# One semaphore increment per accumulation group instead of one per matmul, in a fused attention and feed-forward block

## The chip, the cores and the metric

The kernel runs on one core of a Trainium2 chip. The metric is the device time of one execution in microseconds; a quoted time is the median of several executions. Single looks (one execution) have no state of their own and are used only for distances inside their traces.

Distances between instructions are differences of start times in the instruction records of the trace. They are whole nanoseconds, so I give means.

## The reference, cut to what matters

```python
# x: 2048 x 1024; 32 query heads of 128, 4 key/value heads, the last 512 keys; F = 3584
mod = silu(c) @ w_mod                      # six vectors of 1024: sa, ca, ga, sb, cb, gb
h = layernorm(x) * (1 + ca) + sa
q = h @ wq;  p = softmax(q @ k^T * 128**-0.5);  o = p @ v
x = x + ga * (o @ wo)
h = layernorm(x) * (1 + cb) + sb
x = x + gb * ((silu(h @ w_gate) * (h @ w_up)) @ w_down)
```

## The kernel before

The kernel is written by hand, in program order per engine. A small tracker inserts every wait: each operation on an engine increments that engine's semaphore, and a buffer remembers the count at which it was last written and read. An engine that needs the buffer waits for that count.

```python
def op(self, st, emit, reads=(), writes=()):
    ...                                   # req: the counts that the buffers ask for
    for s, c in req.items():
        if s is st and st.self_exempt:    # TensorE does not wait for itself
            continue
        if synced.get(s, 0) >= c:
            continue
        eng.wait_ge(s.sem, c)
        synced[s] = c
    ins = emit()
    st.count += st.inc
    c = st.count
    ins.then_inc(st.sem, st.inc)
    for b in reads:
        b.reads[st] = c
    for b in writes:
        b.last_write = (st, c)
        b.reads = {}
```

All matmuls go through one helper, which is why nearly all of TensorE's work has one line number (L266) in the profile:

```python
def mm(out_ap, lhsT, rhs, start, stop, reads, bank_buf, skip=False):
    T.op(PE, lambda: TE.matmul(out_ap, lhsT, rhs, start=start, stop=stop, skip_group_check=skip),
         reads=reads, writes=[bank_buf])
```

The groups that the argument touches: the modulation at the start (one-column matmuls, a new weight each, accumulated over eight steps `k`), the scores (four matmuls that are whole groups by themselves), and P@V (groups of four, 129 columns: V and a column of ones that gives the softmax's denominator).

```python
# modulation, first half of the columns; later read by a copy on DVE
for k in range(kh * HK, (kh + 1) * HK):
    for pt in range(2):
        for j in range(HK):
            o = pt * HK + j
            mm(bank(XB, 1, 2 * o), w[:, k, j * P:(j + 1) * P], sc_bf[:, k:k + 1],
               k == 0 and o == 0, k == DT - 1, ...)
...
# scores of one head, then two exponentials of 128x1024 on ACT
for kt in range(KT):
    mm(bank(SCB + kt), kT_sb[:, gk * KT + kt, :], qT_s[qs], True, True, ...)
...
# P@V of one head; rows of v_aug are VW = 130 elements, 260 B, apart
for j in range(TPC):
    for kt in range(KT):
        mm(bank(b, P + 1, (j % 2) * 130), ex_s[es][:, kt, j * P:(j + 1) * P],
           v_aug[:, gk * KT + kt, 0:P + 1], kt == 0, kt == KT - 1, ...)
```

The Q and output projections and the feed-forward part are groups of 8, 32, 8 and 28 matmuls of 512 columns.

The softmax here doesn't subtract the row's maximum and nothing guards it: scores larger than these inputs give would overflow.

Of the kernel before, what the change touches and what calls it, by code (L numbers as in the profile page):

```python
# [39 lines left out]
class _Tracker:  # L40
# [11 lines left out]
            self.issuer_synced[key] = d  # L52
        return d

    def op(self, st, emit, reads=(), writes=()):
        req = {}
        for b in reads:
            lw = b.last_write
            if lw is not None:
                s, c = lw  # L60
                if req.get(s, 0) < c:
                    req[s] = c
        for b in writes:
            lw = b.last_write
            if lw is not None:
                s, c = lw
                if req.get(s, 0) < c:
                    req[s] = c
            for s, c in b.reads.items():
                if req.get(s, 0) < c:  # L70
                    req[s] = c
        synced = self._synced(st)
        eng = st.issuer
        for s, c in req.items():
            if s is st and st.self_exempt:
# [3 lines that stand above are left out]
            eng.wait_ge(s.sem, c)  # L79
            synced[s] = c  # L80
        ins = emit()
        st.count += st.inc
        c = st.count
        ins.then_inc(st.sem, st.inc)
        for b in reads:
            b.reads[st] = c
        for b in writes:
            b.last_write = (st, c)
            b.reads = {}
        return c  # L90
# [40 lines left out]
def bass_adaLN_cond__sliding_block_cached__swiglu_ffn__prompt_kernel(  # L131
# [124 lines left out]
    with nc.Block() as block:  # L256

        @block.gpsimd
        def _(g):
# [4 lines left out]

            def mm(out_ap, lhsT, rhs, start, stop, reads, bank_buf, skip=False):
                T.op(PE, lambda: TE.matmul(out_ap, lhsT, rhs, start=start, stop=stop, skip_group_check=skip),  # L266
                     reads=reads, writes=[bank_buf])

            def transpose(out_ap, in_ap, reads, bank_buf):
                T.op(PE, lambda: TE.transpose(out_ap, in_ap, ident),  # L270
# [12 lines left out]
            def finish(gen):  # L283
                while gen in bg:
# [6 lines left out]
                 reads=[B_ident], writes=[B_ident])  # L291
# [78 lines left out]
            for gk in range(Hkv):  # L370
                T.op(Q_k[gk], lambda: SP.dma_start(k_nat[:, gk * KT:(gk + 1) * KT, :],
                                                   A_k_cache[0, gk, Sk - W:Sk, :].rearrange("(p k) d -> p k d", p=P)),
                     writes=[B_kn[gk]])
            load_wq(1)
            for gk in range(Hkv):
                T.op(Q_v[gk], lambda: SP.dma_start(v_aug[:, gk * KT:(gk + 1) * KT, 0:P],
                                                   A_v_cache[0, gk, Sk - W:Sk, :].rearrange("(p k) d -> p k d", p=P)),
                     writes=[B_vg[gk]])
# [55 lines left out]
            def mod_mm(w_ap, wbuf, k, cols):  # L434
                for n, (j, o) in enumerate(cols):
                    mm(bank(XB, 1, 2 * o), w_ap[:, j * P:(j + 1) * P], sc_bf[:, k:k + 1],
                       k == 0 and n == 0, k == DT - 1, [wbuf, B_sc], PB[XB], skip=True)
# [10 lines left out]
            def warm(n, b):  # L448
                for _ in range(n):
                    mm(bank(b), zwarm[:, 0:P], zwarm, True, True, [B_zw], PB[b])  # L450
# [27 lines left out]
            def mod_slice(sl, kh):  # L478
                for k in range(kh * HK, (kh + 1) * HK):
                    for pt in range(2):  # L480
                        w = wme[sl][pt]
# [3 lines that stand above are left out]
                               k == 0 and o == 0, k == DT - 1, [B_wme[sl][pt][kh], B_sc], PB[XB], skip=True)  # L485
# [4 lines left out]
                 reads=[B_x[tl]], writes=[B_ns4[tl], B_acc])  # L490
            T.op(POOL, lambda: g.tensor_scalar(nmean[:, :], acc[:, 0:1], -1.0 / D, None, op0=ALU.mult),
                 reads=[B_acc], writes=[B_nm])
            T.op(ACT, lambda: A.activation(nsc4[tl], x_res[:, tl, :], AF.Square, bias=nmean[:, 0:1], accum_out=acc[:, 1:2]),
                 reads=[B_x[tl], B_nm], writes=[B_ns4[tl], B_acc])
# [10 lines left out]
                 reads=[B_acc], writes=[B_rs[tl]])  # L505
            T.op(POOL, lambda: g.tensor_tensor(rstd[tl][:, :], rstd[tl][:, :], mhalf[:, 0:1], ALU.pow),
                 reads=[B_rs[tl], B_mh], writes=[B_rs[tl]])
            T.op(POOL, lambda: g.tensor_tensor(nmr[:, :], nmean[:, :], rstd[tl][:, :], ALU.mult),
                 reads=[B_rs[tl], B_nm], writes=[B_nr])
            T.op(ACT, lambda: A.activation(nsc4[tl], x_res[:, tl, :], AF.Identity, bias=nmr[:, 0:1], scale=rstd[tl][:, 0:1]),  # L510
                 reads=[B_x[tl], B_nr, B_rs[tl]], writes=[B_ns4[tl]])
# [373 lines left out]
```

## Time and profile before

| | |
|---|---|
| time, median of 3 | 1291.36 us (1290.51 to 1291.66) |
| matmuls in the program | 7778: 5226 of 512 columns, 2048 of 129, 384 of one, 56 of 256, 64 of 128 |
| start-to-start distance, 512 columns | 215.8 ns |
| 256 columns | 109.2 ns |
| 129 columns (P@V) | 58.6 ns: 56.0 after the first of a group, 59.2 to 60.1 after the others |
| one column (modulation) | 25.6 ns |

The page of the kernel before opens with the span and the busy time of each engine. "PEld" is TensorE's weight load, which runs beside the matmuls.

```profile
span 1290.8 us, 17912 instructions
...
PE 1265.6 (98%) x7636; PEld 651.7 (50%) x7778; DVE 447.7 (35%) x823; ACT 341.3 (26%) x384; POOL 37.3 (3%) x94
```

PE is busy nearly all the time, but matmuls overlap in their pipeline, so that alone doesn't say that they run at their own pace. The groups of TensorE instructions, with shapes kept apart (columns: line, engine, operation, output and input, array and shape, count; busy us and mean ns of one; idle time before them and what ended it):

```profile
L266 PE MATMUL ps<-arena 128*128 128x512 bf16 x5084 | 1134.8, 380 | 10.9 <-DVE arena L467 2.2 <-ACT arena L620 0.6 <-DVE tmp L657 0.4
L266 PE MATMUL ps<-arena 128*128 128x129 bf16 x2048 | 140.6, 220 | 1.1 <-DVE arena L638 1.1
L266 PE MATMUL ps<-sc_bf,arena 128*128 128x1 bf16 x384 | 11.5, 164 | 0.0
```

A matmul of 512 columns lasts 380 ns, yet the next one starts 215.8 ns later. (142 of the 5226 have no record.) The distances times the counts give about 1269 us. The list of what TensorE waited for (total us, times, longest) is short:

```profile
PE ps L270 <- DVE nsc L399: 10.2, 1, 10.2
PE ps L266 <- DVE arena L467: 2.2, 2, 1.7
PE ps L266 <- DVE arena L638: 1.1, 1, 1.1
PE ps L266 <- ACT arena L620: 0.6, 2, 0.4
PE ps L266 <- DVE tmp L657: 0.4, 1, 0.4
```

The chain of work that ended last, in order of time (start, us, what): a piece of the start, where the second half of the modulation ends and DVE reads it; one of attention; and two of the feed-forward part.

```profile
23.23 1.48 PE ps L266 x33
24.74 0.17 DVE mod_bf L440
...
295.35 7.00 PE ps L266 x55
...
703.96 10.74 PE ps L266 x49
714.75 10.74 PE ps L266 x49
```

From one feed-forward piece to the next, 10.79 us pass for 50 matmuls: 215.8 ns each. The chain is TensorE all the way, so a change pays only if it changes the pace of matmuls or one of the few waits above.

### The profile page before, as it was taken

The numbers are of one execution on the slowest core, as the hardware profiler recorded it, in microseconds if no ns is written. First come the engines' busy times: TensorE is split into PE (matmuls) and PEld (weight loads), VectorE is DVE, ScalarE is ACT, GpSimd is POOL, SyncE is SP. The second block draws the span as 40 slices with busy tenths as digits, with TensorE's granted clock in tenths as the row PEclk, the third lists the DMA queues.
The fourth block names the chain that finished last, engine by engine and source line by source line (L and its number), as shares of the span: only waits on it lengthen the run. The fifth ranks groups of instructions, "written<-read, shape, count | busy, mean of one in ns | idle before, by whom it ended". The sixth has DMA issues, their size and how long they took to land.

```text
span 1290.8 us, 17912 instructions
## 1 busy us (share of the span) xinstructions
PE 1265.6 (98%) x7636; PEld 651.7 (50%) x7778; DVE 447.7 (35%) x823; ACT 341.3 (26%) x384; POOL 37.3 (3%) x94
## 2 busy tenths in 40 slices
PE   6999999999999999999999999999999999999999
PEld 3565545556445564456544444444444444444444
DVE  3455423654136542265422332233222331221222
ACT  2555402555015551055620111001100111001100
POOL 1001200000000000000000000000000000000000
PEclk9999999999999999999999999999999999999999
DMA  8989800844105541046340683045420564044300
GB/s 261 304 222 285 235 1 21 184 111 107 37 5 127 133 118 46 1 116 122 70 152 15 205 302 131 17 130 162 151 71 19 157 208 131 17 135 142 131 9 25
DMA packets 212592, 155.33 MB, mean 120 GB/s; under 512 B 104736, under 2 KB 199840, under 8 KB 211488
## 3 DMA queue, kind: packets, MB, share of 16 engines
q1 hardware_dynamic: 212512, 154.17, 42.4%
q8 instruction: 61, 1.00, 0.3%
q14 instruction: 19, 0.16, 0.0%
HBM read 125.83 MB, written 4.19 MB: 101 GB/s over the span
## 4 chain that ended last, share of the span: by engine, by line
PE 97%; issue 1%; DVE 1%; ACT 0%; DMA 0%; SPq 0%; POOL 0%; ACTq 0%
PE ps L266 97%; DMA x_res<-in_A_x_dram 0%; ACT arena L620 0%; PE ps L270 0%; DVE tmp L657 0%; DVE arena L467 0%; DVE st L388 0%; ACT L620 0%; ACT arena L489 0%; SPq L309 0%; DVE nsc L399 0%; DVE arena L638 0%; DVE x_res L659 0%; ACT arena L593 0%; DVE rl L635 0%
## 5 line engine op out<-in xcount | busy, mean ns | idle before, releaser
L266 PE MATMUL ps<-arena 128*128 128x512 bf16 (+1 forms) x7204 | 1251.5, 333 | 12.0 <-DVE arena L467 2.2
L266 PEld LDWEIGHTS ps<-arena 128*128 128x128 bf16 x7346 | 637.4, 98 | 624.9 <-issue 7.9
L620 ACT ACTIVATE arena<-ps 128x1024 bf16<-128x1024 f32 x256 | 261.7, 1023 | 358.9 <-PE ps L266 347.2
L815 ACT ACTIVATE arena<-ps 128x512 bf16<-128x512 f32 x112 | 66.9, 597 | 514.5 <-PE ps L266 511.6
L816 DVE TENSOR_TENSOR arena<-ps,arena 128x512 bf16<-128x512 f32 x112 | 77.5, 692 | 276.2 <-PE ps L266 276.2
L657 DVE TENSOR_TENSOR tmp<-ps,rowb 128x512 f32<-128x512 f32 (+1 forms) x65 | 44.4, 683 | 320.5 <-PE ps L266 320.5
L571 DVE CAST arena<-ps 128x512 bf16<-128x512 f32 x124 | 85.8, 692 | 65.5 <-PE ps L266 65.5
L638 DVE TENSOR_TENSOR arena<-ps,rl 128x512 bf16<-128x512 f32 x128 | 88.5, 691 | 4.4
L635 DVE RECIPROCAL rl<-ps 128x4 f32<-128x4 f32 x128 | 23.4, 183 | 149.7 <-PE ps L266 149.7
L388 DVE BATCH_NORM_STATS2 st<-x_res 128x6 f32<-128x512 bf16 x62 | 42.4, 684 | 4.3 <-DMA x_res<-in_A_x_dram 4.2
L393 POOL TENSOR_SCALAR rstd<-mv 128x1 f32<-128x1 f32 x31 | 7.0, 227 | 955.2 <-DVE mv L392 943.7
L659 DVE TENSOR_TENSOR arena<-tmp,x_res 128x512 bf16<-128x512 f32 (+1 forms) x33 | 22.3, 676 | 1.1
L659 DVE TENSOR_TENSOR x_res<-tmp,x_res 128x512 bf16<-128x512 f32 x32 | 22.1, 692 | 1.1
L404 DVE TENSOR_SCALAR arena<-arena,gain,mod_bf 128x512 bf16<-128x512 bf16 x56 | 20.4, 406 | 0.0
L395 POOL TENSOR_TENSOR rstd<-rstd,mhalf 128x1 f32<-128x1 f32 x31 | 17.7, 572 | 2.6
L399 DVE TENSOR_SCALAR nsc<-x_res,mv,rstd 128x1024 bf16<-128x1024 bf16 x30 | 16.1, 536 | 2.1 <-POOL rstd L395 2.1
L270 PE MATMUL ps<-arena,nsc 128*128 128x128 bf16 x16 | 2.1, 311 | 10.4 <-DVE nsc L399 10.2
L266 PEld LDWEIGHTS ps<-sc_bf,arena 128*128 128x128 bf16 x384 | 11.3, 97 | 0.5
L266 PE MATMUL ps<-sc_bf,arena 128*128 128x1 bf16 x384 | 11.5, 164 | 0.0
L540 POOL TENSOR_SCALAR arena<-arena,c 128x128 bf16<-128x128 bf16 x16 | 9.7, 621 | 36.0 <-PE ps L266 35.9
L392 DVE BATCH_NORM_AGGREGATE mv<-st 128x2 f32<-128x12 f32 x31 | 6.5, 209 | 1.1
L270 PEld LDWEIGHTS ps<-arena,nsc 128*128 128x128 bf16 x16 | 1.5, 142 | 10.4 <-DVE nsc L399 10.4
(37 smaller groups left out, 30.9 us busy)
## 6 DMA issues: line engine op xcount, KB each, us to landing
arena<-in_A_wq_dram SPq DMA_DIRECT2D x31, 1024.0 KB, 5.9
arena<-in_B_w_gate_dram SPq DMA_DIRECT2D x28, 1024.0 KB, 5.3
arena<-in_B_w_up_dram SPq DMA_DIRECT2D x28, 1024.0 KB, 7.4
arena<-in_w_mod_dram SPq DMA_DIRECT2D x8, 1024.0 KB, 7.2
arena<-in_A_wo_dram SPq DMA_DIRECT2D x8, 1024.0 KB, 8.2
arena<-in_B_w_down_dram SPq DMA_DIRECT2D x7, 1024.0 KB, 6.3
arena<-in_w_mod_dram SPq DMA_DIRECT2D x8, 512.0 KB, 7.8
out_dram<-arena SPq DMA_DIRECT2D x15, 256.0 KB, 2.0
```

What stands on the lines that cost most here:

```text
L266: T.op(PE, lambda: TE.matmul(out_ap, lhsT, rhs, start=start, stop=stop, skip_group_check=skip), reads=reads, writes=[bank_buf])
L388: T.op(DVE, lambda: V.bn_stats(st_[sl][:, hf * 6:hf * 6 + 6], x_res[:, t, hf * 512:hf * 512 + 512]), reads=[B_x[t]], writes=[B_st[sl]])
L395: T.op(POOL, lambda: g.tensor_tensor(rstd[sl][:, :], rstd[sl][:, :], mhalf[:, 0:1], ALU.pow), reads=[B_rs[sl], B_mh], writes=[B_rs[sl]])
L404: T.op(DVE, lambda: V.tensor_scalar(dst[:, dt, :], dst[:, dt, :], gain[gi][:, dt:dt + 1], mod_bf[:, ccol + dt:ccol + dt + 1], op0=ALU.mult ...
L571: T.op(DVE, lambda: V.tensor_copy(qT_s[qs], bank(QB)), writes=[PB[QB], B_qT[qs]])
L620: T.op(ACT, lambda: A.activation(ex_s[es][:, 2 * kp:2 * kp + 2, :], banks2(SCB + 2 * kp), AF.Exp, scale=att_scale), writes=[PB[SCB + 2 * k ...
L635: T.op(DVE, lambda: V.reciprocal(rl[r][:, :].rearrange("p (a b) -> p a b", a=2), psap(PVB * 512 + P, [[512, 2], [130, 2]])), writes=both + ...
L638: T.op(DVE, lambda: V.tensor_tensor(o_s[os_].rearrange("p (a b) d -> p a b d", a=2), psap(PVB * 512, [[512, 2], [130, 2], [1, P]]), rlb, A ...
L657: T.op(DVE, lambda: V.tensor_tensor(tmp[s][:, 0:n], bank(b, n), rowb[ri][:, c0:c0 + n], ALU.mult), reads=[B_row[ri]], writes=[PB[b], B_tmp ...
L659: T.op(DVE, lambda: V.tensor_tensor(dst[:, c0:c0 + n], tmp[s][:, 0:n], x_res[:, t, c0:c0 + n], ALU.add), reads=[B_tmp[s], B_x[t]], writes= ...
L815: T.op(ACT, lambda: A.activation(sg_s[ss], bank(gb), AF.Silu), writes=[PB[gb], B_sg[ss]])
L816: T.op(DVE, lambda: V.tensor_tensor(guT[:, ft, :], bank(ub), sg_s[ss], ALU.mult), reads=[B_sg[ss]], writes=[PB[ub], B_gu[ft]])
```

## The change

The intent: engines that read PSUM need to know only that a group has ended, so only its last matmul has to signal. The others lose their increment. An operation that depends on an inner matmul gets the count that the next signalling matmul will reach.

```diff
-    def op(self, st, emit, reads=(), writes=()):
+    def op(self, st, emit, reads=(), writes=(), signal=True):
 ...
         ins = emit()
-        st.count += st.inc
-        c = st.count
-        ins.then_inc(st.sem, st.inc)
+
+        c = st.count + st.inc
+        if signal:
+            st.count = c
+            ins.then_inc(st.sem, st.inc)
 ...
                T.op(PE, lambda: TE.matmul(out_ap, lhsT, rhs, start=start, stop=stop, skip_group_check=skip),
-                     reads=reads, writes=[bank_buf])
+                     reads=reads, writes=[bank_buf], signal=stop)
```

The order of instructions is the same on every engine; a few waits fall away or move to a later count.

## The prediction

> **What bounds the kernel now.** TensorE's issue rate. The page's busy table gives PE 1265.6 us of a 1290.8 us span; the chain of work that ended last is 97% matmuls; the table of waits of PE sums to 15 us, 10.2 of them one wait for the first LayerNorm. The granted clock is 1.00. Busy time does not tell the pace, so I took start-to-start distances from the instruction records: 215.8 ns for 512 columns, 109.2 for 256, 58.6 on average for the 129 columns of P@V (56 after a group's first matmul, 59 to 60 after the others), 25.6 for the one-column modulation matmuls. Counting 5226, 56, 2048, 384 and 64 of them (7778) gives about 1269 us; the rest is start-up, the last evacuation and short waits.
>
> **What the change does.** It takes the increment off 6231 of 7778 matmuls (by my count 1547 stay, among them all score matmuls, all transposes and one in four of P@V). No instruction is added or moved on any engine. A reader of a group's inner matmul now waits for the next signalling matmul: that touches the diagonal tiles on POOL (up to 3 matmuls later), the reuse of the late modulation weights (loaded some ten heads later) and the DMA transposes after an output projection (behind P@V matmuls that come later anyway). Evacuations waited for a group's last matmul before too. None of this is on the chain.
>
> **What an increment can cost.** From 256 to 512 columns, 106.7 ns for 256 columns is 0.4167 ns a column, so all fixed cost of a 512-column matmul is about 2.5 ns. If all of it were the increment: 6231 x 2.5 ns = 16 us (1.2%). The 3 ns more of P@V's inner matmuls could add 1536 x 3 ns = 5 us, but first and later matmuls of a group signal alike, so that is hardly the signal. The Trainium skill ("TensorE: Matmul & The Clock Gate", "Back-to-back issue gap") states N/2.4 + 2.5 ns for warm matmuls and about 25 ns as an issue floor at small N; both match here (215.8 and 25.6 ns). The same page ("The cost: per-tile semaphore tail") states that increments serialize at 26.3 ns each. At 56 to 216 ns between matmuls no queue builds up; only the one-column matmuls, at 25.6 ns, could be limited by it. They hold 384 x 25.6 ns = 10 us; if half went, 5 us. I think the floor there is issue, and expect nothing.
>
> **Predicted time.** 1290.6 us, 8 in 10 between 1286.0 and 1292.5. Faster by over 2%: 0.02; within 2%: 0.97; slower by over 2%: 0.01.
>
> **What would show it.** Right: the chain's pieces of 49 matmuls still take 10.74 us; 16 P@V matmuls still 0.94 us; 32 one-column matmuls in the start still 0.83 us; PE's waits are the same; groups are evacuated as soon after their end as before. Wrong: the 512-column distance falls toward 213.3 ns (pieces of 10.6 us), P@V to 56 ns throughout, or the one-column ones well below 25 ns.
>
> **What would make it wrong.** An increment that holds the matmul pipeline (up to 16 to 21 us faster, evenly over the kernel); increments that delay later ones on their way to the evacuating engines (then the few exposed waits at the start, before the first softmax and at the end shrink, 1 to 2 us); or a later threshold that delays a DMA that I think is early (slower, a new wait of PE on a DMA).

## The result, and the profile after

The changed kernel took 1292.09 us (median of 4, 1291.47 to 1293.02), against 1291.09 us of the kernel before in the same rounds (median of 4: the three above and 1290.83). The ratio of after to before is 1.0008, with a 95% interval from 0.9991 to 1.0026: the same. (Ratios and intervals come from runs of both kernels in the same rounds, so a ratio is not quite the ratio of the medians.) Five more rounds, below, gave 1.0000 with 0.9987 to 1.0014.

The page's opening lines after:

```profile
span 1289.7 us, 17906 instructions
...
PE 1264.9 (98%) x7636; PEld 651.4 (51%) x7778; DVE 447.6 (35%) x823; ACT 341.5 (26%) x384; POOL 37.4 (3%) x94
```

The increments did go: the trace of the PE semaphore holds 7779 updates before and 1548 after, one more than the counts of signalling matmuls (7778 and 1547) in both. The groups of TensorE instructions after, line numbers two higher because of the diff:

```profile
L268 PE MATMUL ps<-arena 128*128 128x512 bf16 x5084 | 1134.0, 380 | 10.7 <-DVE arena L469 1.9 <-ACT arena L622 0.6 <-DVE tmp L659 0.4
L268 PE MATMUL ps<-arena 128*128 128x129 bf16 x2048 | 140.6, 220 | 1.1 <-DVE arena L640 1.1
L268 PE MATMUL ps<-sc_bf,arena 128*128 128x1 bf16 x384 | 11.5, 164 | 0.0
```

What TensorE waited for, after:

```profile
PE ps L272 <- DVE nsc L401: 10.1, 1, 10.1
PE ps L268 <- DVE arena L469: 1.9, 2, 1.5
PE ps L268 <- DVE arena L640: 1.1, 1, 1.1
PE ps L268 <- ACT arena L622: 0.6, 2, 0.4
PE ps L268 <- DVE tmp L659: 0.4, 1, 0.4
```

The same places of the chain, after:

```profile
22.35 1.23 PE ps L268 x33
23.61 0.17 DVE mod_bf L442
...
294.22 7.00 PE ps L268 x55
...
702.83 10.74 PE ps L268 x49
713.62 10.74 PE ps L268 x49
```

The reader should see two things. First, nothing in the steady part moved: the same 7.00 and 10.74 us, the same P@V total of 140.6 us. From the first P@V matmul to the start of the last matmul of the kernel, 1249.956 us pass before and 1249.963 after. Of the 6231 removed increments 6077 lie in this stretch, and four further traces, of kernels that differ only in the signals at the start or in P@V's width, take 1249.960 to 1249.967 us for it. So an increment cost it less than 0.01 ns. Second, one thing did move: the wait on DVE's line L467 (L469 after), whose longest went from 1.7 to 1.5 us, and the piece of the chain in front of the modulation's copy, from 1.48 to 1.23 us. In the records the copy starts 463 and 516 ns after the last one-column matmul (for the two halves) before, and 255 and 265 ns after. The gap of TensorE there shrank from 1.877 to 1.625 us.

That is a gain of 0.25 us on the chain, and the times can't show it: across the traces the first P@V matmul starts anywhere from 35.5 to 37.8 us. This scatter is larger than all differences between these two kernels. It goes with the clock granted at the start (0.50 from 24.0 to 27.3 us in the trace of the run "late" below, for instance): by trace, 6 to 16 of the 512-column matmuls there are 427 ns apart instead of 216. With 0.211 us for each of these taken off, as an estimate, the time from the first matmul to the first P@V matmul is 24.38 and 24.39 us in the two traces whose modulation matmuls all signal, and 24.0 to 24.2 in nine of the other ten (the tenth has 24.6, with 0.4 us of wait on a load).

### The profile page after: what moved, and what is told of

The parts are those of the page before. It is cut to its first block, busy times and chain, and to the rows that moved or that the text cites. A ratio compares the mean times of both kernels' runs of the same rounds, so it can differ in the third digit from the quotient of the medians.

```text
span 1289.7 us, 17906 instructions
## 1 busy us (share of the span) xinstructions
PE 1264.9 (98%) x7636; PEld 651.4 (51%) x7778; DVE 447.6 (35%) x823; ACT 341.5 (26%) x384; POOL 37.4 (3%) x94
## 4 chain that ended last, share of the span: by engine, by line
PE 97%; issue 1%; DVE 1%; ACT 0%; DMA 0%; SPq 0%; POOL 0%; ACTq 0%
PE ps L268 97%; DMA x_res<-in_A_x_dram 0%; ACT arena L622 0%; PE ps L272 0%; DVE tmp L659 0%; DVE arena L469 0%; DVE st L390 0%; ACT L622 0%; ACT arena L491 0%; SPq L311 0%; DVE nsc L401 0%; DVE arena L640 0%; DVE x_res L661 0%; ACT arena L595 0%; DVE rl L637 0%
```

## The experiments

Theory: an increment costs the matmul stream nothing, because increments are carried out beside it, one after the other. Only where matmuls come faster than increments can be carried out does a queue form, and then the engine that waits for the last one starts late. In this kernel that is so only for the one-column matmuls. (The part on the queue of one-column matmuls came with the first probe below; the expectations before it have only the first sentence.)

Rivals: an increment holds the stream by part of the 2.5 ns that a matmul takes beyond its columns; the increments that were left hold the cost; later counts delay something that offsets a gain.

No run doubles the cost with a second increment on each matmul. The increment was measured by itself instead.

### The changed kernel in more rounds

No edit.

> The changed kernel again, in more rounds, to narrow the interval. Theory (an increment costs the matmul stream nothing): ratio to before within 0.998 to 1.002, and in the records the same distances as before, 215.8 ns for 512 columns and 878 ns for 15 steps of P@V. Rival (an increment holds the stream by up to 2.5 ns): 6231 fewer of them would save up to 16 us, ratio down to 0.988. Second rival (later thresholds delay something): a wait of PE that before does not have, and a ratio over 1.002.

Measured: 1291.42 us (median of 5) against 1291.83 (median of 9) of before, ratio 1.0000, interval 0.9987 to 1.0014. The stretch from the first P@V to the last matmul took 1249.964 us, the copy's delays were 255 and 265 ns. The first rival asked for up to 16 us; it falls, and so does the second.

### Fewer increments still

```diff
 mm(bank(SCB + kt), kT_sb[:, gk * KT + kt, :], qT_s[qs], True, True, ...,
+   sig=kt % 2 == 1)
 ...
 mm(bank(b, P + 1, (j % 2) * 130), ex_s[es][...], v_aug[...], kt == 0, kt == KT - 1, ...,
+   sig=j == TPC - 1 and kt == KT - 1)
```

> The change taken further: of the score matmuls only each second signals, of the 16 P@V matmuls of a head only the last, so that about 900 increments stay instead of 1547. No wait ends later. Theory: same time as before and as the changed kernel, ratio 0.998 to 1.002, same distances. Rival (what the increments cost sits in those that the change left, the ones at the ends of the groups where engines wait): the time falls by at least 1 us and the softmax and the P@V read-out start sooner after their matmuls than the 200 ns after the next matmul's start that both kernels show.

Measured: ratio 1.0001 (0.9989 to 1.0014), and 1250.02 us from the first P@V to the last matmul. The reciprocal that reads P@V starts 198 ns after the start of the matmul that follows the group, as before; so the increments that the change left hold no cost either. (TensorE's list of waits has one entry more here, 0.4 us on a load of modulation weights at 13.6 us, before any matmul that this edit touches.)

### A signal too late

```diff
 mm(bank(SCB + kt), kT_sb[:, gk * KT + kt, :], qT_s[qs], True, True, ...,
+   sig=kt == KT - 1)
```

> The changed kernel, but the four score matmuls of a head signal only at the fourth, so the first exponential of a head waits for two more matmuls than it needs, 2 x 216 ns = 0.43 us. Theory (the place of a signal matters only where the wait is exposed): in the steady loop the exponentials start 0.43 us later and PE does not wait; only before the first P@V and around the last heads, where before's chain goes through the exponentials, does PE lose some 0.4 us each: 0.5 to 1.5 us in all, ratio 1.000 to 1.002. Rival (the exponential is close to critical in every head): 128 x some 0.1 to 0.4 us, 13 to 50 us slower.

Measured: ratio 1.0000 (0.9988 to 1.0013). The first P@V to the last matmul took 1250.333 us, 0.37 us more. The chain of this kernel near the last heads, where no Q projection fills TensorE's time any more, shows where:

```profile
636.50 2.55 PE ps L268 x11
639.05 0.02 issue
639.07 1.03 ACT arena L622
640.11 0.02 issue
640.13 1.03 ACT arena L622
641.16 0.05 issue
641.21 3.27 PE ps L268 x26
```

Two exponentials stand in the chain here; the kernel before had one (1.03 us at 641.77). In the other heads the exponentials start 0.43 us later and nobody waits for them. So the place of a signal can cost something where the number of signals does not, but in this kernel only at one place. My expectation of 0.5 to 1.5 us was a little high: the wait before the first P@V did not grow.

### The modulation matmuls alone, and all but them

The first kernel is before with this part of the change alone, the second is the changed kernel without it. (Both ran after the first probe of the next section.)

```diff
 # before, every matmul signals, except here:
 mm(bank(XB, 1, 2 * o), w[:, k, j * P:(j + 1) * P], sc_bf[:, k:k + 1],
-   k == 0 and o == 0, k == DT - 1, ...)                  # signals
+   k == 0 and o == 0, k == DT - 1, ..., sig=k == DT - 1)
```
```diff
 # the changed kernel, where only the ends of groups signal, except here:
-   k == 0 and o == 0, k == DT - 1, ...)                  # signals if k == DT - 1
+   k == 0 and o == 0, k == DT - 1, ..., sig=True)
```

> The kernel before with one part of the change alone: the 128 one-column modulation matmuls at the start signal only in the last round over the contraction, all others signal as before. Theory (what the change gains is the queue of increments behind these matmuls and nothing else): the copy that reads the modulation starts 255 and 265 ns after the last one-column matmul's start, as in the changed kernel, where before has 463 and 516; the gap of PE after them is 1.63 us, not 1.88; all from the first P@V matmul to the last matmul takes 1249.96 us, as in both. Rival (the gain there comes from other increments, of the transposes or warm-up matmuls around): 463 and 516 ns stay.

> The other half: the changed kernel, but the 128 one-column modulation matmuls at the start all signal again. Theory: delays of 463 and 516 ns and the PE gap of 1.88 us come back, and the rest takes 1249.96 us. Rival: 255 and 265 ns, 1.63 us.

Measured, one look each:

| | before | after | modulation alone | all but modulation |
|---|---|---|---|---|
| copy after last one-column matmul, first half | 463 ns | 255 | 255 | 465 |
| second half | 516 ns | 265 | 265 | 515 |
| TensorE's gap there | 1.877 us | 1.625 | 1.624 | 1.873 |
| first P@V to last matmul | 1249.956 us | 1249.963 | 1249.967 | 1249.964 |

TensorE's wait there in the list of waits (total, times, longest), with the modulation part alone:

```profile
PE ps L268 <- DVE arena L469: 1.5, 1, 1.5
```

and with all but the modulation part:

```profile
PE ps L268 <- DVE arena L469: 1.7, 1, 1.7
```

All that the change gains, it gains with 112 of its 6231 increments. The other 6119 gain nothing that these traces resolve. Each of the two kernels has a single trace, but the same 254 or 255 and 264 or 265 ns stand in all nine other traces in which these matmuls signal only at the end.

### The increment by itself

After the kernel's last matmul come batches of small matmuls on data that happens to lie in SBUF. Each batch follows full matmuls without signals, and a copy on DVE waits for its last matmul.

```diff
+for kind in ("col", "tile"):
+    for every in (True, False):
+        ...                                        # 10 matmuls of 512 columns, sig=False
+        for n in range(64):                        # "col"; "tile": 16 matmuls on 32x32 tiles, 128 columns
+            mm(bank(0, 1, n), wd_s[:, 2, 0:P], wd_s[:, 3, n:n + 1], True, True, ...,
+               sig=every or n == 63)
+        T.op(DVE, lambda: V.tensor_copy(dst, src), writes=...)
```

> Measures the increment by itself. After the kernel's last matmul come 12 batches (3 times 4 kinds), each after ten full matmuls without a signal: 64 one-column matmuls where each signals, the same where only the last does, 16 matmuls on 32 x 32 tiles of the array (128 columns) where each signals, and the same where only the last does. A copy on DVE waits for the last one. The kernel is some 33 us longer; outputs stay right. Theory (increments leave the issue of matmuls alone): same distances with and without, about 25.6 ns for one column. For the copy's delay after the last matmul's start there are two theories. Increments queue at 26.3 ns each, as the skill's page on TensorE states: with 16 tile matmuls a few ns apart the copy starts some 350 to 400 ns later where each signals than where only the last does, and about the same for the 64 one-column matmuls, whose 25.6 ns distance nearly keeps up (up to 64 x 0.7 = 45 ns later). Increments don't queue: under 30 ns difference in both.

Measured, with the same numbers within 2 ns in three repetitions:

| batch | first to last start | copy after last start, each signals | last alone signals | difference |
|---|---|---|---|---|
| 64 one-column matmuls | 1.58 us | 780 ns | 201 ns | 579 ns |
| 16 tile matmuls | 50 ns | 723 ns | 337 ns | 386 ns |

The order of DVE's copies in the second repetition shows it directly (one column each, one column last, tile each, tile last):

```profile
1305.04 0.16 DVE L878 COPY tmp<-ps 128x4 f32<-128x4 f32 x1 [4.19 <-PE ps L268]
1308.22 0.16 DVE L878 COPY tmp<-ps 128x4 f32<-128x4 f32 x1 [3.02 <-PE ps L268]
1311.07 0.16 DVE L878 COPY tmp<-ps 128x4 f32<-128x4 f32 x1 [2.68 <-PE ps L268]
1313.15 0.16 DVE L878 COPY tmp<-ps 128x4 f32<-128x4 f32 x1 [1.92 <-PE ps L268]
```

TensorE needs 10 x 215.8 + 64 x 25.1 = 3764 ns for the second batch, but only 3.18 us pass between the first two copies: the first one came 0.58 us late.

The Trainium skill ("TensorE: Matmul & The Clock Gate", "The cost: per-tile semaphore tail") states that increments of tile matmuls serialize, with a tail of 26.3 ns per increment. The tile batch agrees: 386 / 15 = 25.7 ns of delay for each increment that was added. But I had expected nearly nothing for one column, since 26.3 hardly exceeds the distance of 25.1 ns, and it was 579 ns. That expectation failed, and the next kernel asks why.

```diff
+# kinds: one column, 8 to 128 matmuls; 32 matmuls of 32 to 129 columns; tiles, 4 to 16 matmuls
+BATCHES = ([("col", 1, n) for n in (8, 16, 32, 64, 128)]
+           + [("col", w, 32) for w in (32, 64, 72, 80, 96, 129)]
+           + [("tile", 128, n) for n in (4, 8, 16)])
+...
+# and 16 matmuls as in P@V, signal at the end alone: 128, 129, 129 not accumulated, 112, 96 columns
```

> The increment by itself once more, after the kernel's last matmul, every batch after 14 full matmuls without a signal, once with each signalling, once with only the last. From the first probe: 64 one-column matmuls delayed the copy by 580 ns, so an increment takes (1581 + 580) / 63 = 34.3 ns; 16 tile matmuls delayed it by 386 ns, so (50 + 386) / 15 = 29.1 ns. Theory (one increment at a time, 29 to 34 ns each, in a queue that does not hold the matmuls): the delay of one-column matmuls grows by 9.2 ns a matmul, some 65, 140, 285, 580 and 1165 ns at 8, 16, 32, 64, 128, with the distances unchanged; of 32 matmuls, some 285 ns at 32 columns, 30 to 160 ns at 64 (29 ns apart), under 70 at 72, none (under 10 ns) at 80, 96 and 129; tiles 75 to 90 at 4, 180 at 8, 386 at 16. Rivals: a queue of bounded depth (the delay stops growing, and the distances grow with increments and not without); a fixed latency of signals after a busy spell (delay the same at 8 and 128). The last five batches measure the pace of P@V alone, no increments: 16 matmuls in groups of four, 128, 129, 129 without accumulation, 112 and 96 columns. If accumulation costs the 3 ns, 59 falls to 56 in the third; if another instruction, say the weight load, paces them, the distance stays over 55 at 112 and 96 columns.

| batch | distance | copy later by, when each signals |
|---|---|---|
| one column, 8 matmuls | 25.4 ns | 70 ns |
| one column, 16 | 25.2 ns | 143 ns |
| one column, 32 | 25.2 ns | 288 ns |
| one column, 64 | 25.1 ns | 579 ns |
| one column, 128 | 25.1 ns; 34 to 35 for the last 31 when each signals | 878 ns, and the batch 285 ns longer |
| 32 columns, 32 matmuls | 25.1 ns | 283 ns |
| 64 columns | 29.1 ns | 155 ns |
| 72 columns | 32.4 ns | 51 ns |
| 80 columns | 35.7 ns | 2 ns |
| 96 columns | 42.5 ns | 1 ns |
| 129 columns | 58.2 ns | 1 ns |
| tiles, 4, 8, 16 matmuls | 3.3 ns | 79, 180, 387 ns |

One number explains the rows: an increment takes 34.2 ns. A matmul that comes after 25.1 ns adds 9.2 ns to the queue (579 / 63), one after 32.4 ns adds 1.7 (51 / 31), and at 35.7 ns and more there is no queue. The queue is bounded: with 128 matmuls the distances jump from 25 to 34 ns after 97 of them, and from then on the increment does hold the matmul stream. At that point 97 x (1 - 25.1 / 34.2), some 26 increments, were waiting; that depth is an estimate from these distances. 285 + 878 = 1163 ns is what the 9.2 ns a matmul gives, so the work is the same and only its place changes. A fixed latency after a busy spell falls, since the delay grows with the count.

The traces show the queue without any sum, too, because they hold the time of every update of the PE semaphore. Wherever increments queue, its updates are 34 or 35 ns apart, 34.2 in the mean: behind the one-column matmuls of the probes, behind those of the modulation in the kernel before, and behind the tiles. In the probes and in the modulation the copy starts 22 to 24 ns after the last update. The sum for the tiles in the expectation above, (50 + 386) / 15 = 29 ns, missed this because it took the starts of the tile matmuls for their ends: where the last one alone signals, its update comes 263, 297 and 364 ns after the first start with 4, 8 and 16 tiles, so 8.4 ns a tile. An increment that takes 34.2 ns then delays the copy by 25.8 ns a tile, which is 387 / 15.

In the kernel before, 32 one-column matmuls stand together in front of each of the two copies. The probe says 288 ns for that; the kernel showed 208 and 251. The difference is accounted for: the changed kernel still signals at the last eight, which queue too, so that its copies start 54 and 64 ns later than the probe's 201. Against 201 ns the kernel before was late by 262 and 315.

### The 3 ns in P@V

The prediction left a loose end: why all but the first matmul of a P@V group take some 3 ns longer. Two tries missed before one hit.

```diff
-mm(bank(b, P + 1, (j % 2) * 130), ..., v_aug[:, gk * KT + kt, 0:P + 1], ...)
+mm(bank(b, VW, (j % 2) * VW), ..., v_aug[:, gk * KT + kt, 0:VW], ...)      # 130 columns, even
```

> The changed kernel with the P@V matmuls 130 columns wide instead of 129 (the last one, ones like the 129th, is not read). It asks what the 3 ns are by which all but the first of a P@V group take longer, with or without increments. If an odd number of columns costs them, the distance is 56.7 ns throughout and the kernel 3 to 4 us faster than before (ratio 0.997). If accumulation costs them, 59.6 ns stay, and 0.4 ns x 2048 make it about 1 us slower. Neither has to do with the increments; the theory that increments are free expects no difference of first and later matmuls between this and the same kernel with increments.

Measured: ratio 1.0001 (0.9989 to 1.0014), the same distances to the nanosecond (56 and 59 to 60): neither an even width nor more columns mattered. The last five batches of the probe of widths cleared accumulation: 56.7 ns at 129 columns with it and without. The weight load does not pace them either: 42.5 ns at 96 columns. In that probe the rows of the moving operand were aligned. In the kernel they are 260 B apart, and sorting the distances by the row's start address, only the starts at multiples of 16 B (0, 1040, 2080 and 3120 B) were fast (56.0 ns), which are the first of each group.

```diff
-            VW = 130
+            VW = 160        # rows 320 B apart; the other kernel has 136: 272 B
```

> The changed kernel with the rows of V and its ones column 320 B apart in SBUF instead of 260 B, nothing else. In before's records the P@V matmuls whose moving operand starts at a multiple of 16 B (0, 1040, 2080, 3120 B: the first of each group) take 56.0 ns, those at other starts 59.2 to 60.1 ns, with increments and without, at 129 and 130 columns; the probe's P@V batches, with aligned rows, ran at 56.6 ns with and without accumulation. If the start address is the cause, all go at 56 to 57 ns: 1536 x some 3 ns = 4 to 5 us, ratio 0.9955 to 0.9975, 1245.5 us from the first P@V to the last matmul instead of 1249.96. If it is the place in the group, nothing changes.

> The same with 272 B, a multiple of 16 B but not of 32 or 64 B. If 16 B decides, as the first matmuls of the groups at 1040 and 3120 B say, the same 56 to 57 ns and the same 4 to 5 us as with 320 B. If a multiple of 64 B is needed for the rows as a whole, the distance stays at 59 to 60 ns for most and the time nearer to before's.

Measured: 1287.82 us with 320 B (median of 5; before 1292.22, median of 9), ratio 0.9965, interval 0.9953 to 0.9978; 1287.84 us with 272 B, ratio 0.9970, interval 0.9957 to 0.9984. All P@V distances are 56.7 ns. The group of P@V matmuls with 320 B, to be held against the 140.6 us above:

```profile
L268 PE MATMUL ps<-arena 128*128 128x129 bf16 x2048 | 137.0, 220 | 1.1 <-DVE arena L640 1.1
```

The 3.6 us come back in the stretch from the first P@V to the last matmul, 1246.36 us in both kernels against 1249.96. That is less than the 4 to 5 us expected, because the fast distances became 56.7 ns and not 56.0. So the start address is the cause, and a multiple of 16 B is enough. Which other starts are slow stays open: in P@V a start 8 B past a multiple of 16 took 59.2 ns, but in the probe's batch of 32 matmuls with 129 columns, where the starts of the operand and of the output wander, such a start took 56.0 ns, like a multiple of 16, and only the others took 59 to 60. The Trainium skill ("Advanced Engine Details and Errata", "SBUF Cachelines") states that SBUF has cachelines of 16 bytes; that fits the P@V distances, but how the matmul's read meets them is argued here, not shown, and the probe's fast starts at 8 B speak for more than this one rule. The kernel with 320 B is better than both kernels of this case, by 0.35%. That is still inside the 2% that counts as the same.

## Why the prediction was right, point by point

- The time, 1290.6 us with 1286.0 to 1292.5, held the 1292.09 us. There is some luck in it: the median lay 0.4 us under the range's end and one of the four runs, 1293.02 us, beyond it. The 1.0 us between the medians of the two kernels is scatter; five more rounds gave 1.0000. "I think the floor there is issue, and expect nothing" came out: 1.0000 in the rounds with the narrower interval.
- "What bounds the kernel now": right. The distances are the same to 0.1 ns after the change, and where they did change (320 B rows), the time followed.
- "No instruction is added or moved", later counts are harmless: right. The list of TensorE's waits has the same five entries after.
- "All fixed cost of a 512-column matmul is about 2.5 ns. If all of it were the increment: 16 us": the bound was right (by the table's distances the 106.7 ns should read 106.6, which changes nothing), and the increment's part of it is nothing that the trace resolves. The skill's N/2.4 + 2.5 ns ("TensorE: Matmul & The Clock Gate", "Back-to-back issue gap") gives 215.8 ns for 512 columns; this case has 215.8 with increments and without.
- "At 56 to 216 ns between matmuls no queue builds up": right, shown by the probe from 80 columns (35.7 ns) upwards.
- "Only the one-column matmuls, at 25.6 ns, could be limited by it ... if half went, 5 us": their distance stayed at 25.6 ns without increments, so increments don't set that floor, as said. But the prediction took the skill's 26.3 ns for the time of an increment, hardly more than 25.6; with the measured 34.2 ns the increments queue behind these matmuls without slowing them, and the copy that waits for the last one was late by 208 and 251 ns. The prediction had that among its risks, "1 to 2 us" over several exposed waits. It was 0.25 us at one: the waits before the first softmax and at the end of the kernel follow matmuls that are too far apart for a queue.
- "Groups are evacuated as soon after their end as before" holds for all groups but these: the copy of Q starts 201 ns after the next matmul's start in both kernels, the reciprocal 198 ns.
- "That is hardly the signal" about P@V's 3 ns: right, and the cause was the start address.

## What to carry to other kernels

Removing semaphore increments from matmuls is worth nothing while the matmuls start further apart than an increment takes (34.2 ns here; between the 72 and 80 columns of the probe for a whole-array matmul); it is worth doing where many small or packed matmuls come in a burst and another engine waits for their end, at up to 9 ns a matmul at one column and 26 ns a tile. Look at the distance of starts first, then at who waits behind the burst. And when some matmuls of one shape are a few nanoseconds slower than others, sort them by the start address of the moving operand: padding rows to a multiple of 16 B took 3.6 us out of this kernel, and the change 0.25.

## What the Trainium skill lacked or had wrong

- "TensorE: Matmul & The Clock Gate", "The cost: per-tile semaphore tail", has the queue of increments for packed tiles alone. Here whole-array matmuls build one too, below 34 to 36 ns from start to start: 579 ns behind 64 one-column matmuls. It also lacks that the queue is bounded and then holds the matmuls (34 to 35 ns instead of 25 after 97 of them). And its 26.3 ns is one term of a tail, beside 4.7 ns for each tile, and not the time of an increment, for which it is easily taken: the updates of the tile batches were 34.1 ns apart. The two terms together fit: 31.0 ns a tile, against 30.8 here ((724 - 355) / 12).
- "Advanced Engine Details and Errata", "DMA Bandwidth Details", states about one cycle as an increment's overhead on trn2, in a list on DMA and without saying whose increment or what it delays. It has no figure for a matmul's: 34.2 ns here when it queued, and otherwise nothing that the distances of the matmuls resolve. Whether the two are the same quantity is not shown.
- "TensorE: Matmul & The Clock Gate", "Back-to-back issue gap": its table gives about 60 cycles (25 ns) for 1 to 64 columns; 64 columns took 29.1 ns here, which is its own N/2.4 + 2.5. Its figures for streams of weight load and matmul, 81 ns at 128 columns and 131 ns at 512, don't fit here: 55.8 ns at 128 columns (837 / 15, in the probe of widths) and 215.8 at 512, each matmul with its own weight load.
- "SBUF — State Buffer", "Operand start alignment", is about what is legal and says that it timed nothing. No page that I found has what a start address costs a matmul: 59.2 to 60.1 ns instead of 56.7 ns at 129 columns in P@V where the moving operand did not start at a multiple of 16 B.
